# Loading decays whole, queries and keys in two pieces, and four parts of a weight check slice by slice

## The chip, the cores and the metric

One core of a Trainium2 chip runs the whole program. The metric is device time in microseconds for one execution. Lower is better.

## The reference

An attention layer with a complex decay feeds a two-layer network. For each batch, head and time step a state of 48 by 48 is turned and shrunk by the decay, the outer product of key and value is added, and the query reads it:

```python
mag = np.sqrt(a_re * a_re + a_im * a_im)
scale = np.minimum(mag, 0.999) / (mag + 1e-06)
a_re_n, a_im_n = (a_re * scale, a_im * scale)
for t in range(S):                       # S = 768, B = 4, H = 8, D = 48
    new_re = ar * S_re - ai * S_im       # ar, ai: a_re_n, a_im_n at t
    new_im = ar * S_im + ai * S_re
    S_re, S_im = (new_re + kv, new_im)   # kv: outer product of k and v at t
    y[:, :, t] = np.einsum('bhd,bhde->bhe', q[:, :, t], S_re)
h = x @ w_in                             # x: y as 3072 tokens by 384; w_in: 384 x 2048
out = np.maximum(0.01 * h, h) @ w_out    # w_out: 2048 x 384
```

## The kernel before, in words

The recurrence is cut into 12 sub-chunks (`SUBS`) of 128 time steps for two of the four batches. For sub-chunk n the kernel does this:

- `fetch_a(n)` loads the decays (768 KB, two planes: real and imaginary), `fetch_qk(n)` loads the queries and keys (768 KB, two planes), `fetch_v(n)` the values (832 KB). All loads are issued by SP, in one queue.
- `prep(n)` turns decays into running products on ScalarE and VectorE. Its first step is a square of the decays on ScalarE (line 719). Later VectorE multiplies queries and keys by the products into the tile `qkt` (lines 842 and 906).
- `relay_of(n, 0)` and `relay_of(n, 1)` move the queries and then the keys from `qkt` to `t96`, each with five DMAs from SBUF to SBUF, issued by SP (the key relay only after the last step of `prep(n)`).
- `attend(n)` works on TensorE: the scores (many small matmuls, 96 rows by 32 columns of weights), a mask on VectorE, then the product with the values, and the update of the state.

The two-layer network (`forward`) runs between these on TensorE, in groups of 256 tokens: `first` (18 matmuls into `ph`), leaky relu and split on ScalarE and VectorE (`hide`, `halve`), `second` (matmuls into `po`). Its weights come in 64-bit words, and `convert` splits them in the first 90 us.

A last job is `check_weights(i)`: it loads all weights once more, in 11 parts of three slices (part 10 has two), each slice 128 x 384 words of 8 bytes, that is 384 KB, and ScalarE squares them and sums exponentials. The result decides at the end whether a general version has to run. The parts use the two buffers of the tag "a", which the decays used. Part 0 needs `prep(10)` done, part 1 needs `prep(11)`, and part i needs part i - 2 (line 615); so in time the order of loads is 0, 2, 4, 6 and then 1, 8, 3, 10, 5, 7, 9.

The order of instructions on each engine is not written by hand. `drive` simulates the tasks with the cost functions (`dma_cost`, `act_cost` and so on) and picks, for each lane, the task that can start first, by rank. `Lane` then ties each instruction to the one before it on its engine. For a load cut in pieces the kernel replaces the log entries of the pieces by one entry of the whole load (`spq.log[-2:] = [...]`).

`in_turn` (line 579) adds a true wait: the load waits on SP until the load before it in the list `loaded` has landed. `pieces` (line 585) cuts a load into its two planes and puts both in turn; for n < 1 it loads in one piece with no wait. `fetch_a(n)` calls it with n - 1, so that the decays of sub-chunks 0 and 1 come whole and those from 2 on in two; `fetch_qk` cuts from sub-chunk 1 on. Each part of the check is one load of 1152 KB, in turn. While SP waits, everything behind in its queue waits too.

Of the kernel before, what the change touches and what calls it, by code (L numbers as in the profile page):

```python
# [21 lines left out]
P = 128  # L22
# [117 lines left out]
def in_sbuf(x):  # L140
    return x.space == bass.MemoryType.SB
# [42 lines left out]
def dma_cost(name, kw, aps):  # L184
    if name == "memset":
        return 0.3, 0.4
    out = kw["out"]
    if in_sbuf(kw["in_"]) and in_sbuf(out):
        return 0.78, 2.75
    each = out.nbytes() / 400e3  # L190
    return max(each, 0.6), each + 2.4
# [270 lines left out]
def body(ctx, tc, keep, a_in, qk_in, v_in, w_in, out):  # L462
# [26 lines left out]
    spq, plq = Lane(tc, nc.sync, dma_cost), Lane(tc, nc.gpsimd, dma_cost)  # L489
# [15 lines left out]
        out=perm[:, 0].rearrange("p (x r j) -> p x r j", x=NB, r=R),  # L505
        in_=perm[:, 0].rearrange("p (x r j) -> p x r j", x=NB, r=R),
# [3 lines left out]
        out=perm[:, 1].rearrange("p (r j x) -> p r j x", r=R, j=JB),  # L510
        in_=perm[:, 1].rearrange("p (r j x) -> p r j x", r=R, j=JB),
# [28 lines left out]
    a_off = [0]  # L540
# [35 lines left out]

    loaded = []

    def in_turn(x):
        if loaded:  # L580
            landed = mybir.DependencyInfo(mybir.DependencyClass.Sync, mybir.DependencyReason.DATA)
            tc.add_manual_dep(x.ins, loaded[-1], landed, reason="load")
        loaded.append(x.ins.name)

    def pieces(out, in_, n):
        if n < 1:
            spq.dma_start(out=out, in_=in_)
            return
        for l in range(2):
            in_turn(spq.dma_start(out=out[:, l], in_=in_[:, l]))  # L590
        spq.log[-2:] = [dma_cost("dma_start", dict(out=out, in_=in_), [])]

    def fetch_a(n):
        yield "S", *([prepared[n - 2], moved_k[n - 2]] if n > 1 else freed(A) if n else []), *([loading[n - 1]] if n else [])
        N = TI * len(SUBS[n][1]) * C
        loading[n].set(0.0)
        raw_a[n] = a = a_0 if n == 0 else pp.tile([P, 3, N], F32, tag="a", name=f"a_{n}", bufs=2)
        pieces(a[:, 1:3], a_in[a_off[n] : a_off[n + 1]].rearrange("(p l x) -> p l x", p=P, l=2), n - 1)

    def fetch_qk(n):  # L600
        yield "S", *([prepared[n - 1], moved_k[n - 1]] if n else [])
        N = TI * len(SUBS[n][1]) * C
        raw_qk[n] = qk = pp.tile([P, 2, N], F32, tag="qk", name=f"qk_{n}")
        pieces(qk, qk_in[a_off[n] : a_off[n + 1]].rearrange("(p l x) -> p l x", p=P, l=2), n)

    def fetch_v(n):
        yield "S", *(attends_of(n - 1) if n else freed(V))
# [6 lines left out]
    def check_weights(i):  # L614
        yield "S", checked[i - 2] if i > 1 else prepared[nsub - 2 + i]
        s0 = i * WCK
        ns = min(WCK, NWC - s0)
        st = pp.tile([P, WCK, DM], I64, tag="a", name=f"wck_{s0}", bufs=2)
        in_turn(spq.dma_start(out=st[:, :ns], in_=w_in[s0 : s0 + ns].rearrange("s p x -> p s x")))
        words = st.rearrange("p s x -> p (s x)").bitcast(F32).rearrange("p (x two) -> p x two", two=2)  # L620
        lo, hi = words[:, : ns * DM, 0], words[:, : ns * DM, 1]
        yield "A"
        act.activation(lo, hi, AF.Square)
        yield "A"
        act.activation(hi, lo, AF.Exp, scale=-65536.0, accum_out=wacc[:, 1, i : i + 1])
        yield "A"
        act.activation(lo, lo, AF.Exp, scale=40.0, bias=big, accum_out=wacc[:, 0, i : i + 1])

    def freed(*places):
        return [x for x, r in zip(converted, ROUND) if r in places]  # L630
# [723 lines left out]
    for n in range(nsub):  # L1354
        fetched_a[n] = task(fetch_a(n), UNIT[0] + 5.5 * UNIT[1] if n == 1 else R_RELAY + 0.5)
        fetched_qk[n] = task(fetch_qk(n), R_HID if n else UNIT[0] + 2.5 * UNIT[1])
        prepared[n] = task(prep(n), *due(n))
        if n == 0:
            for i in range(NU):
                converted.append(task(convert(i), UNIT[0] + i * UNIT[1]))  # L1360
        fetched_v[n] = task(fetch_v(n), R_RELAY - 1 if n else UNIT[0] + 9.5 * UNIT[1])
        moved_q[n] = task(relay_of(n, 0), R_RELAY)
        moved_k[n] = task(relay_of(n, 1), R_RELAY)
        attended[n] = task(attend(n), R_ATT)
    forwarding = task(forward(), R_FF)
    for i in range(-(-NWC // WCK)):
        checked[i] = task(check_weights(i), R_WCK)
# [87 lines left out]
```

## Time and profile before

| | |
|---|---|
| median of 3 runs | 602.8 us (602.29 to 603.14) |
| the profiled execution | 602.46 us |
| its span in the trace | 600.8 us |
| busy: TensorE (PE), VectorE (DVE), ScalarE (ACT) | 92%, 86%, 66% of the span |
| instruction queue q8 over the span | 61 packets, 1.00 MB |

The span is the time from the first to the last instruction in the trace, so some 1.7 us of the execution lie around it. PE is TensorE's matmuls and PEld its weight loads. SP is the engine that issues nearly all DMAs. "hardware_dynamic" is the queue of data moves that engines issue, and "instruction" those that bring instructions to the engines. "idle ... <-X" says what ended a wait of an engine, and "issue" is time in which it waited for nothing that the profile shows. A releaser can be misattributed when an engine waits for several things.

### The profile page before, as it was taken

Reading aid. Unit: us, or ns where it says so; the run is one execution under the profiler, and the core shown is the slowest. Engines: PE = TensorE matmul, PEld = TensorE weight load, DVE = VectorE, ACT = ScalarE, POOL = GpSimd, SP = SyncE. Lnnn points to the kernel's source line nnn. Section 1 sums busy time; section 2 is a strip of 40 time slices with the busy share of each in tenths; the row PEclk is TensorE's granted clock in tenths of the full one; section 3 lists DMA queues with packets and bytes.
Section 4 is the critical chain, followed back from the end, with each engine's and each line's share of the span. In section 5 each row is a group of like instructions: output and inputs, shape, how many; then the busy total and the mean of one; then the engine's idle time right before and its main releaser. Section 6 shows DMA issues by size and latency. Waiting matters only on the chain.

```text
span 600.8 us, 17929 instructions
## 1 busy us (share of the span) xinstructions
PE 553.6 (92%) x7667; PEld 525.7 (88%) x7667; DVE 514.8 (86%) x880; ACT 399.3 (66%) x882; POOL 5.0 (1%) x23
## 2 busy tenths in 40 slices
PE   3761798999999999999999999999999998999994
PEld 2420488999999999999999999999999998999994
DVE  5999989999889999999999989999999987965232
ACT  7987487495485784582684864764754854687973
POOL 2000000000000000000000000000000000000000
PEclk9995899999999999999999999999999998999998
DMA  8952535325343245223434353153135245446740
GB/s 349 407 190 82 159 96 145 111 70 148 82 137 86 77 138 134 86 80 87 123 89 118 103 132 108 60 132 107 59 80 153 81 123 195 176 138 208 238 159 29
DMA packets 31428, 79.21 MB, mean 132 GB/s; under 512 B 3568, under 2 KB 9712, under 8 KB 31344
## 3 DMA queue, kind: packets, MB, share of 16 engines
q1 hardware_dynamic: 31200, 77.89, 42.7%
q8 instruction: 61, 1.00, 0.7%
q14 instruction: 23, 0.19, 0.1%
q10 hardware_dynamic: 144, 0.13, 0.1%
HBM read 54.26 MB, written 4.72 MB: 98 GB/s over the span
## 4 chain that ended last, share of the span: by engine, by line
PE 83%; DVE 5%; issue 1%; ACT 1%; ACTq 0%; DVEq 0%
PE po L125 33%; PE ph L125 33%; PE att L125 17%; DVE qkt L125 2%; DVE a L125 1%; DVE u L125 1%; DVE stage_st L125 0%; ACT wck L125 0%; DVE stage_hid L125 0%; DVE qk L125 0%; DVE stage_stg L125 0%; DVE scr L125 0%; DVE hid L125 0%; DVE tg L125 0%; ACT ot L125 0%
## 5 line engine op out<-in xcount | busy, mean ns | idle before, releaser
L125 PE MATMUL po<-hid,wout_hi 128*128 128x256 f32 x1152 | 217.4, 281 | 1.8 <-ACT hid L125 1.4
L125 PE MATMUL ph<-x,win_hi 128*128 128x256 f32 x1152 | 217.2, 280 | 0.0
L125 PEld LDWEIGHTS po<-hid,wout_hi 128*128 128x128 f32 x1152 | 182.1, 189 | 6.1 <-issue 3.3
L125 PEld LDWEIGHTS ph<-x,win_hi 128*128 128x128 f32 x1152 | 182.1, 188 | 1.3 <-ACT hid L125 0.4
L125 PE MATMUL ph<-x,win_lo 128*128 128x256 f32 x576 | 142.1, 278 | 0.0
L125 PE MATMUL po<-hid,wout_lo 128*128 128x256 f32 x576 | 139.0, 279 | 0.0
L125 PEld LDWEIGHTS po<-hid,wout_lo 128*128 128x128 f32 x576 | 109.0, 189 | 0.2
L125 PEld LDWEIGHTS ph<-x,win_lo 128*128 128x128 f32 x576 | 108.6, 189 | 0.3
L125 ACT ACTIVATE tg<-ph 128x512 f32<-128x512 f32 x96 | 57.2, 596 | 66.6 <-PE ph L125 64.1
L125 DVE TENSOR_TENSOR tg<-ph,tg 128x512 f32<-128x512 f32 x81 | 55.7, 688 | 30.5 <-ACT tg L125 30.1
L125 DVE TENSOR_TENSOR hid<-tg,hid 128x512 fp32r<-128x512 f32 x81 | 55.6, 687 | 16.5 <-ACT hid L125 16.4
L125 ACT CAST hid<-tg 128x512 fp32r<-128x512 f32 x81 | 49.7, 615 | 25.6 <-DVE tg L125 25.6
L125 DVE TENSOR_TENSOR u<-a 128x384 f32<-128x384 f32 x84 | 46.6, 555 | 1.8 <-ACT a L125 0.4
L125 DVE TENSOR_TENSOR qkt<-qk,a 128x768 f32<-128x768 f32 x48 | 44.5, 953 | 0.1
L125 ACT ACTIVATE rst<-rst,t 96x48 f32<-96x48 f32 x160 | 37.6, 322 | 4.8 <-DVE rst L125 4.8
L125 PE MATMUL att<-t 96*32 96x128 f32 (+3 forms) x1536 | 34.8, 250 | 2.5 <-issue 2.1
L125 PEld LDWEIGHTS att<-t 96*32 96x32 f32 x1536 | 32.4, 144 | 2.6 <-DMA t<-qkt 1.0
L125 PE MATMUL att<-asb,v 128*32 128x128 f32 x592 | 34.2, 285 | 0.0
L125 PE MATMUL att<-t,rst 96*32 96x128 f32 x640 | 33.3, 272 | 0.0
L125 ACT ACTIVATE sq<-a 128x1536 f32<-128x1536 f32 x12 | 17.9, 1489 | 22.6 <-DMA a<-in_a_dram 22.6
L125 ACT ACTIVATE wck<-wck 128x1152 f32<-128x1152 f32 (+1 forms) x22 | 27.0, 1229 | 8.4 <-DMA wck<-in_w_dram 8.3
L125 DVE TENSOR_TENSOR a<-u 128x192 f32<-128x192 f32 x84 | 29.9, 356 | 1.8
(167 smaller groups left out, 797.1 us busy)
## 6 DMA issues: line engine op xcount, KB each, us to landing
t<-qkt SPq DMA_DIRECT2D x48, 290.2 KB, 4.2
wck<-in_w_dram SPq DMA_DIRECT2D x10, 1152.0 KB, 5.6
v<-in_v_dram SPq DMA_DIRECT2D x12, 832.0 KB, 4.5
qk<-in_qk_dram SPq DMA_DIRECT2D x22, 384.0 KB, 3.1
a<-in_a_dram SPq DMA_DIRECT2D x20, 384.0 KB, 3.5
out_dram<-ot SPq DMA_DIRECT2D x11, 384.0 KB, 2.7
t<-qkt SPq DMA_DIRECT2D x24, 129.0 KB, 4.1
stage_st<-in_w_dram SPq DMA_DIRECT2D x3, 768.0 KB, 6.5
```

Of the source, the lines that this page charges most:

```text
L125: x = getattr(self.engine, name)(*args, **kw)
```

## The change

The decays of every sub-chunk are loaded whole, with no wait, and noted in `loaded`. The queries and keys stay in two pieces from sub-chunk 1 on; each waits until the load noted last has landed, and is then noted itself. Of the check, parts 0 to 3 are loaded in single slices, each of which waits until the load two places before it in `loaded` has landed, so that two are in flight. Parts 4 to 10 are loaded whole with no wait but that for their buffer.

```diff
-    def in_turn(x):
-        if loaded:
+    def behind(x, k):
+        if len(loaded) >= k:
             landed = mybir.DependencyInfo(mybir.DependencyClass.Sync, mybir.DependencyReason.DATA)
-            tc.add_manual_dep(x.ins, loaded[-1], landed, reason="load")
+            tc.add_manual_dep(x.ins, loaded[-k], landed, reason="load")
         loaded.append(x.ins.name)
-
-    def pieces(out, in_, n):
-        if n < 1:
-            spq.dma_start(out=out, in_=in_)
-            return
-        for l in range(2):
-            in_turn(spq.dma_start(out=out[:, l], in_=in_[:, l]))
-        spq.log[-2:] = [dma_cost("dma_start", dict(out=out, in_=in_), [])]
 
     def fetch_a(n):
...
-        pieces(a[:, 1:3], a_in[a_off[n] : a_off[n + 1]].rearrange("(p l x) -> p l x", p=P, l=2), n - 1)
+        x = spq.dma_start(
+            out=a[:, 1:3], in_=a_in[a_off[n] : a_off[n + 1]].rearrange("(p l x) -> p l x", p=P, l=2)
+        )
+        loaded.append(x.ins.name)
 
     def fetch_qk(n):
...
-        pieces(qk, qk_in[a_off[n] : a_off[n + 1]].rearrange("(p l x) -> p l x", p=P, l=2), n)
+        src = qk_in[a_off[n] : a_off[n + 1]].rearrange("(p l x) -> p l x", p=P, l=2)
+        if n:
+            for l in range(2):
+                behind(spq.dma_start(out=qk[:, l], in_=src[:, l]), 1)
+            spq.log[-2:] = [dma_cost("dma_start", dict(out=qk, in_=src), [])]
+        else:
+            spq.dma_start(out=qk, in_=src)
...
-        in_turn(spq.dma_start(out=st[:, :ns], in_=w_in[s0 : s0 + ns].rearrange("s p x -> p s x")))
+        src = w_in[s0 : s0 + ns].rearrange("s p x -> p s x")
+        if i < 4:
+            for x in range(ns):
+                behind(spq.dma_start(out=st[:, x], in_=src[:, x]), 2)
+            spq.log[-ns:] = [dma_cost("dma_start", dict(out=st[:, :ns], in_=src), [])]
+        else:
+            spq.dma_start(out=st[:, :ns], in_=src)
```

## Rows read from the trace of the kernel before

**Rows 1.** Page, part 1: busy time, share of the span and instructions of each engine.

```profile
PE 553.6 (92%) x7667; PEld 525.7 (88%) x7667; DVE 514.8 (86%) x880; ACT 399.3 (66%) x882; POOL 5.0 (1%) x23
```

**Rows 2.** All waits of TensorE from 100 to 590 us: total, times, longest.

```profile
PE att L125 <- issue: 2.3, 2, 2.1
```

**Rows 3.** The chain that ended last, near 499 us: start, length, what.

```profile
499.13 2.16 issue
...
501.51 2.86 PE po L125 x12
```

**Rows 4.** The same chain, 36 matmuls of the network in a steady stretch.

```profile
479.39 4.08 PE ph L125 x36
```

**Rows 5.** Stretches: PE, PEld, DVE, ACT, POOL busy; granted clock; DMA share; GB/s.

```profile
501.20:504.40 3.20, 3.11 (x15) 2.96 (x15) 2.72 (x6) 2.95 (x5) 0.00 (x0) 0.50 0.45 136
...
95.10:96.70 1.60, 0.24 (x3) 0.03 (x1) 1.53 (x3) 1.60 (x8) 0.00 (x0) 1.00 0.01 5
96.80:100.00 3.20, 2.83 (x22) 2.63 (x23) 3.08 (x5) 1.58 (x4) 0.00 (x0) 1.00 0.73 165
```

**Rows 6.** DMA queues, 481.5 to 498.8 us, the only queue: packets, MB, share.

```profile
q1 hardware_dynamic: 1439, 2.73, 54.3%
```

**Rows 7.** DMA queues from 498.8 to 499.9 us, the instruction queue.

```profile
q8 instruction: 1, 0.02, 5.4%
```

**Rows 8.** SP's timeline: start and length of issues, tile, source, count.

```profile
423.94 0.33 SPq L125 DMA_DIRECT2D v<-in_v_dram  x1
...
453.72 3.76 SPq L125 DMA_DIRECT2D a<-in_a_dram  x2
...
493.99 0.58 SPq L125 DMA_DIRECT2D wck<-in_w_dram  x1
...
506.34 0.38 SPq L125 DMA_DIRECT2D wck<-in_w_dram  x1
...
539.17 4.00 SPq L125 DMA_DIRECT2D t<-qkt  x5
543.28 17.05 SPq L125 DMA_DIRECT2D wck<-in_w_dram  x4
```

**Rows 9.** DMA queues from 427.9 to 429 us (none before, from 423.9), the instruction queue.

```profile
q8 instruction: 1, 0.02, 5.2%
```

**Rows 10.** DMA queues from 456.6 to 457.7 us (none before, from 453.7), the instruction queue.

```profile
q8 instruction: 1, 0.02, 5.5%
```

**Rows 11.** Page, part 6: DMA issues, KB each, median us from issue to landing.

```profile
v<-in_v_dram SPq DMA_DIRECT2D x12, 832.0 KB, 4.5
qk<-in_qk_dram SPq DMA_DIRECT2D x22, 384.0 KB, 3.1
a<-in_a_dram SPq DMA_DIRECT2D x20, 384.0 KB, 3.5
...
t<-qkt SPq DMA_DIRECT2D x48, 32.2 KB, 2.8
...
wck<-in_w_dram SPq DMA_DIRECT2D x1, 768.0 KB, 4.4
```

**Rows 12.** The chain: the scores of sub-chunk 11.

```profile
546.10 2.74 PE att L125 x93
```

**Rows 13.** Timelines of ScalarE and VectorE from 504 to 515.3 us, three instructions.

```profile
504.03 0.18 ACT L125 ACTIVATION_READ_ACCUMULATOR wck<-wck,low 128x1 f32 x1
512.13 1.27 ACT L125 ACTIVATE wck<-wck 128x1152 f32<-128x1152 f32 x1 [0.60 <-DMA wck<-in_w_dram]
515.29 0.69 DVE L125 TENSOR_TENSOR tg<-ph,tg 128x512 f32<-128x512 f32 x1 [0.84 <-ACT tg L125]
```

**Rows 14.** Waits of ScalarE over the span: total, times, longest.

```profile
ACT sq L125 <- DMA a<-in_a_dram: 22.6, 9, 4.4
```

**Rows 15.** The chain: the scores of sub-chunk 9.

```profile
456.24 3.00 PE att L125 x91
```

**Rows 16.** The chain: 36 matmuls of the network in another stretch.

```profile
301.68 4.24 PE po L125 x36
```

## The prediction before the run

> **What bounds the kernel now.** I read the busy shares first: TensorE works for 92% of the span, more than any other engine [rows 1]. Then its waits from 100 to 590 us, where the change does nearly all its work: there is hardly one but a single stop of 2.1 us that no semaphore ends [rows 2]. So in this stretch a load that lands sooner is worth nothing by itself, and the only things to win are that stop and what hangs on it. The chain puts it at 499.13, inside the scores of sub-chunk 10: 2.16 us of "issue", and behind it 12 matmuls that take 2.86 us [rows 3], where the usual pace is 4.08/36 = 0.113 us each, so 1.36 us [rows 4]. The table by stretches says why those are slow: the granted clock is 0.50 (1.2 of 2.4 GHz) from 501.2 to 504.4, just after the stop [rows 5].
>
> **What the stop is.** TensorE waits for no engine, so I looked at what feeds it. The instruction queue (q8) moves nothing from 481.5 to 498.8, while the data queue is 54.3% busy [rows 6], and its next packet comes in the 1.1 us after that [rows 7]. Check part 0, 1152 KB, had been issued at 493.99 [rows 8]. So TensorE's next instructions moved 4.9 us after that issue, when the part had drained, and TensorE went on at 499.13 + 2.16 = 501.29, some 2.4 us after the block began to move. I read this as a block of instructions queued behind a load on a DMA engine. The same lag shows elsewhere: behind the 832 KB of v issued at 423.94 the block moves at 427.9, 4.0 us later [rows 8, 9]; behind a 384 KB half of the decays issued at 453.72 at 456.6, 2.9 us later [rows 8, 10].
>
> **Part by part.** (The planner's cost of each load is the same before and after, since the log entries are replaced by that of the whole load; so the order on each engine should stay.)
>
> *1. Check part 0 in slices.* Two slices of 384 KB go out at 493.99 and some 0.4 us later, the third when the first has landed, 3.1 to 3.5 us after its issue [rows 11], near 497.3. Behind the waiting third slice SP holds the queries and keys of sub-chunk 11, which waited for the whole part before; that stands within a few tenths. In front of the block lie then 768 KB instead of 1152. No row shows the wait for 768 KB; it lies between 2.9 (384 KB) and 4.0 (832 KB), and since v's landing takes 4.5 and that of the one 768 KB load of the check 4.4 [rows 11] I take 3.8. The block moves at 497.8, TensorE goes on 2.4 later at 500.2: the stop shrinks from 2.16 to 1.1, saved 1.1 us. Ends: 2.0 saved if only the first slice is in front (496.9), 1.3 lost if the block waits for the third slice too (497.3 + 2.9 = 500.2, against 498.9).
>
> *2. The clock behind it.* The 12 matmuls lose 2.86 - 1.36 = 1.5 us [rows 3, 4]. Would a stop of 1.1 us still lower the clock? From 95.1 to 96.7 TensorE was busy 0.24 of 1.6 us and the clock stayed at 1.00 after it [rows 5]. So I take all of it: 1.5 us. Other end: nothing.
>
> *3. How much of 1 + 2 = 2.6 us survives.* TensorE then runs 2.6 us ahead of the other engines. Next in line are the scores of sub-chunk 11 at 546.10 [rows 12]; they need the key relay, whose five moves go out from 539.17 for 4.00 us [rows 8], the last at about 542.6, landing 2.6 to 2.8 later [rows 11], at 545.3: slack 0.8. The relay comes at the end of VectorE's chain, which waits at 515.29 for ScalarE, and ScalarE at 512.13 for check part 2 [rows 13]. Part 2 was issued whole at 506.34 [rows 8]. Now its first slice goes when part 0's last step on ScalarE has freed the buffer, at 504.3 [rows 13]; the second still waits for the second half of the queries and keys, till 506.4; the third goes when the first has landed, 3.1 to 3.5 later, at 507.6, and lands at 511.0, against 512.1. That is 1.1 us sooner, and I add 0.4 for waits that shrink on the way to 539. So the relay gains 1.5, and the scores may start up to 1.5 + 0.8 = 2.3 us sooner: 2.3 of the 2.6 is left.
>
> *4. The decays in one piece.* Ten times a second issue goes and SP no longer sits between the halves, so the decays land 4.4 instead of about 7 us after the issue and the queries follow sooner. What this removes is ScalarE's wait for them, 22.6 us in nine waits [rows 14]; I cost it at nothing, since TensorE shows no wait there [rows 2] and other work of TensorE covers it. But 768 KB instead of 384 now lie before a block of instructions. Where it bites: at 453.72 the block came 2.9 us after the first half and the scores took 3.00 us [rows 10, 15] instead of 2.74 [rows 12], so it was already 0.26 late. With 3.8 it is 0.9 later. This cost is 0 to 0.9 us; most of it would come back out of the stop at 499, whose end is set by a load and not by TensorE. I take 0.2. At the other loads of decays the scores do not stretch, and a block that sat behind the second half (issued 3.4 us later) comes sooner.
>
> *5. The later check parts.* Parts 1 and 3 come as slices after 543.28; parts 4 to 10 go as soon as their buffer is free. ScalarE's order holds the buffer, so there are two in flight at most; TensorE has no wait there [rows 2]: nothing, but see the second rival. Eight more issues on SP of about 0.4 us [rows 8] stand in its idle time. The close behind TensorE's last matmul is unchanged.
>
> **Sum.** 2.3 - 0.2 = 2.1 us off. The profiled execution took 602.46 us (span 600.8 and 1.66 around it), 0.34 below the median of 602.80; so 600.36 for such an execution, 600.7 as a median.
>
> **Rivals.**
> *The block slips in between the slices.* Row: the block did come only when the whole of part 0 had drained [rows 6, 7], but it was one load of 24 rows of 3072 bytes per DMA engine. If each load is an entity, it would now wait for 8 rows: moves at 496.9, TensorE goes on at 499.3, the stop is 0.2 us; 2.0 + 1.5 = 3.5 saved on TensorE, 2.3 to 3.5 behind the relay, say 2.9 and 599.9. The Trainium skill, "DMA: Bandwidth & Descriptors", section "Queues, rings and completion order", says that a DMA engine takes its queues in turn and drains one packet, typically 9 to 17 and at most 64 descriptors, before it goes on to the next. By that rule this rival is right if a slice is a packet; the trace agrees only if all of part 0 was one.
>
> *Part 8 at once, on the other side.* Place: the scores of sub-chunk 11, which eat a block in 2.74 us. Before, part 8 waited for part 1 to land, and the block behind part 1 was in time. Now part 8 (1152 KB) goes 3.7 us after part 1's first slice. If TensorE's request comes after that, the block waits another 4.9 us and moves 8.6 us after the first slice, against some 4 now. The scores start 2 to 2.8 us after that slice (before: 546.10 - 543.28 = 2.8) and run dry at the earliest 2.74 us later [rows 12], so TensorE stands from 5 to 7 until 8.6 + 2.4 = 11: 4 to 6 us, I take 4, and 1.5 for the clock. 602.8 - 2.1 + 5.5 = 606.2. It decides whether the request comes within 3.7 us of the first slice; the request seems to come with the scores' start, so there is a margin of 0.9 us or more, against it.
>
> *Nothing gained.* The stop stays long enough to pull down the clock (third slice in front), or the wait at 457 grows and costs the clock there: 602.8.
>
> *Another pace.* With the clock at 1.00 throughout, 36 matmuls take 4.08 in some stretches and 4.24 in others [rows 4, 16], and I see no cause. Since 471 all run at 4.08. If the 80 us from 510 on flipped, 80 x 0.16/4.08 = 3.1 us would be lost: 602.8 - 2.1 + 3.1 = 603.8. Flips elsewhere can go either way by 1 or 2 us.
>
> **How the numbers follow.** What can be told from no change is 0.2%, 1.2 us. Forecast 0.46, slip between slices 0.20, nothing gained 0.17, part 8 at once 0.07, pace lost 0.10. Faster by over 0.2%: the first two, 0.66. Within: 0.20, the third and some of the last. Slower: 0.14. The range runs from the slip case with all its 3.5 us and a lucky flip of 1 us, 598.3, to near the lost pace, 603.5.
>
> **What would show it.** Right: the stop near 499 shorter than 1.3 us and no stretch at 0.50 after it; the block of instructions moving before 498; scores of sub-chunk 9 near 3.5 to 3.9 us; those of sub-chunk 11 starting about 2 us sooner, perhaps after a short wait for the relay. Wrong: a stop of 2 us or more at 499, at 457 or at 546, or 36 matmuls at 4.24 after 510. ScalarE's waits for the decays should fall from 22.6 to under 10 us without effect on the time.

## The result and the profile after

The change made the kernel slower: 607.29 us as a median of 11 runs (604.18 to 610.92) against 603.23 for the kernel before beside it (602.29 to 605.90), a ratio of 1.0064 with a 95% interval of 1.0039 to 1.0089. That is 3.9 us, three times what can be told from no change; 600.7 had been forecast, and 603.5 was the upper end of the range. The profiled execution is the longest of the 11: 610.92 us with a span of 609.2, 8.4 us above the span before. So its rows show each loss, but some are larger than in a usual run.

TensorE's waits from 100 to 590 us, which answer to [rows 2]:

```profile
PE po L125 <- ACT hid L125: 3.3, 1, 3.3
PE att L125 <- issue: 1.5, 3, 0.8
PE ph L125 <- ACT x L125: 0.7, 1, 0.7
PE ph L125 <- DVE tg L125: 0.5, 1, 0.5
```

The stop of 2.1 us near 499 is gone, and waits for other engines, which were absent, sum to 4.5 us. The table by stretches (columns as in [rows 5]) places the cost behind the longest:

```profile
499.00:504.40 5.40, 5.40 (x75) 5.27 (x78) 4.49 (x10) 1.56 (x2) 0.00 (x0) 1.00 0.37 99
507.00:519.70 12.70, 10.20 (x89) 9.96 (x84) 7.80 (x21) 7.23 (x17) 0.00 (x0) 0.99 0.62 192
519.70:526.50 6.80, 6.00 (x28) 6.00 (x29) 6.80 (x8) 3.34 (x9) 0.00 (x0) 0.51 0.51 176
```

Behind 499 the granted clock now stays at 1.00, where it had been 0.50 [rows 5]. But from 519.7 to 526.5 it is at 0.51 (1.2 GHz), behind a stretch in which TensorE stood for 2.5 of 12.7 us. Here 6.00 us of busy time are about twice what the same work would take at 2.4 GHz, so I estimate 3.0 us lost.

The chain that ended last says where the wait comes from (start, length, what):

```profile
493.77 5.35 DMA wck<-in_w_dram
...
499.14 3.56 DMA wck<-in_w_dram
...
507.31 3.84 DMA wck<-in_w_dram
...
511.18 3.87 DMA wck<-in_w_dram
...
519.94 0.52 ACT hid L125
520.46 0.04 issue
520.50 4.21 PE po L125 x18
```

Each of parts 0 and 2 of the check is two landings one behind the other: the third slice goes out only at 499.14 and 511.18, when the first has landed. The key relay, at the end of VectorE's chain, goes out at 542.51, against 539.17 before [rows 8]. ScalarE works in order, so while it waits for a part it does nothing for TensorE. Its timeline:

```profile
502.81 2.79 ACT L125 ACTIVATE wck<-wck 128x1152 f32<-128x1152 f32 x2 [5.18 <-DMA wck<-in_w_dram]
515.15 2.56 ACT L125 ACTIVATE wck<-wck 128x1152 f32<-128x1152 f32 x2 [4.68 <-DMA wck<-in_w_dram]
```

Before, part 2 was squared from 512.13 after 0.60 us [rows 13], and part 0 came 2.8 us sooner, by the same view of the kernel before:

```profile
500.04 2.58 ACT L125 ACTIVATE wck<-wck 128x1152 f32<-128x1152 f32 x2 [2.25 <-DMA wck<-in_w_dram]
```

A second loss stands where the prediction had put nothing, at the very end. The last piece of the chain is the compare that writes `bad`, and behind it every engine jumps over the general version. The last row of the chain, before:

```profile
597.64 0.15 DVE bad L125
```

and in the changed kernel:

```profile
603.49 0.15 DVE bad L125
```

The DMA queues (packets, MB, share) from that row's end to the end of the span, before:

```profile
q14 instruction: 3, 0.02, 3.1%
```

and in the changed kernel:

```profile
q14 instruction: 4, 0.03, 1.8%
```

The span ends 600.8 - 597.79 = 3.0 us after the compare before, and 609.2 - 603.64 = 5.6 us now: 2.5 us more, with a fourth packet on the second instruction queue, q14. One of the four comes in the last 3.2 us, when the other three are through (the queues from 606 to 609.2):

```profile
q14 instruction: 1, 0.01, 1.0%
```

So the 8.4 us of the two profiles are: 3.7 gained behind 499 (stop and clock, [rows 3, 4]), 4.5 lost in waits, 3.0 in the clock, 2.5 at the close, and 2.1 left over. At least part of that is pace: 18 matmuls take 2.12 us on the changed chain at 534, 0.118 us each, against 0.113 in [rows 4].

```profile
533.98 2.12 PE po L125 x18
```

A third, smaller loss is the stop of 0.8 us inside the scores of sub-chunk 9 at 457.74, behind the decays that now come whole. It is among the "issue" waits above, and so in the 2.1 left over.

### The profile page after: what moved, and what is told of

Read it like the earlier page. It is cut to its first block, busy times and chain, and to the rows that moved or that the text cites. A ratio compares the mean times of both kernels' runs of the same rounds, so it can differ in the third digit from the quotient of the medians.

```text
span 609.2 us, 17911 instructions
## 1 busy us (share of the span) xinstructions
PE 556.0 (91%) x7667; PEld 528.4 (87%) x7667; DVE 514.1 (84%) x880; ACT 400.1 (66%) x882; POOL 5.0 (1%) x23
## 4 chain that ended last, share of the span: by engine, by line
PE 71%; DMA 6%; DVE 6%; ACT 5%; issue 1%; SPq 1%; ACTq 0%; DVEq 0%
PE ph L125 28%; PE po L125 28%; PE att L125 15%; DMA wck<-in_w_dram 5%; ACT wck L125 3%; DVE qkt L125 2%; SPq L125 1%; DMA t<-qkt 1%; DVE a L125 1%; DVE hid L125 1%; DVE tg L125 1%; ACT a L125 0%; ACT tg L125 0%; DVE qk L125 0%; ACT hid L125 0%
## 5 line engine op out<-in xcount | busy, mean ns | idle before, releaser
L125 PE MATMUL att<-t 96*32 96x128 f32 (+3 forms) x1536 | 36.3, 257 | 2.5 <-DMA t<-qkt 1.7
L125 PEld LDWEIGHTS att<-t 96*32 96x32 f32 x1536 | 33.9, 145 | 4.7 <-DMA t<-qkt 2.2
L125 ACT CAST hid<-ph 128x512 fp32r<-128x512 f32 x30 | 17.5, 587 | 15.4 <-PE ph L125 10.3
```

The costliest lines, as they stand in the source:

```text
L125: x = getattr(self.engine, name)(*args, **kw)
```

## The experiments

My theory on seeing this was that the wait between the slices is the whole loss. The rivals: the whole decays; slices as such; the later parts with no wait. All runs were timed against the kernel before on the same chip.

### One half of the change at a time

The fetches as changed, the check as before:

```diff
-        if i < 4:
-            for x in range(ns):
-                behind(spq.dma_start(out=st[:, x], in_=src[:, x]), 2)
...
+        behind(spq.dma_start(out=st[:, :ns], in_=src), 1)
```

> Decays, queries and keys are loaded as in the changed kernel; every part of the check is whole and in turn, as before. Theory (the wait between slices): the loss sits in the check, so this stands within 0.3% of before, 602 to 605 us, with the stop of about 2 us near 499 and the clock at 0.50 behind it still there, and ScalarE's wait for part 2 about 0.6 us. Rival (the whole decays, or what they do to the queries behind them): 606 to 608 us, like the changed kernel, with TensorE waiting for ScalarE near 520.

Measured: 605.84 us, ratio 1.0050 (1.0031 to 1.0070). My theory had 602 to 605, so it fell: most of the loss came without a single slice. The rival's 606 to 608 was missed by little, but TensorE does not wait for ScalarE near 520, so its mechanism was not there either. The stop near 499 with the low clock behind it is there as before. What is new in its profile: a longer stop behind the whole decays and the long close (604.6 - 599.46 = 5.1 us). The chain at 457:

```profile
454.44 2.74 PE att L125 x88
457.18 1.44 issue
458.62 0.32 PE att L125 x3
458.95 1.77 PE ph L125 x9
```

The 9 matmuls behind the stop take 1.77 us, and 1.24 in the run with two pieces below: the clock fell here as well. The DMA queues from 452 to 456.2 us, where this is the only one that moves anything, and those from 456.2 to 457 tell why TensorE stands:

```profile
q1 hardware_dynamic: 308, 0.96, 70.5%
```

```profile
q8 instruction: 1, 0.02, 7.5%
```

The decays were issued at 451.95 and the block of instructions moved only after 456.2, more than 4.2 us later, when they had drained.

The check as changed, the fetches as before:

```diff
-        in_turn(spq.dma_start(out=st[:, :ns], in_=w_in[s0 : s0 + ns].rearrange("s p x -> p s x")))
+        if i < 4:
+            for x in range(ns):
+                behind(spq.dma_start(out=st[:, x], in_=src[:, x]), 2)
...
+        else:
+            spq.dma_start(out=st[:, :ns], in_=src)
```

> Decays, queries and keys are loaded as before, in two pieces in turn; the check is as in the changed kernel. Theory (the wait between slices): nearly the whole loss is here, 605.5 to 608 us; part 0 lands about 9 us after its first slice was issued instead of 6, ScalarE waits 4 to 5 us each for parts 0, 2 and 1, and TensorE waits 2 us or more for ScalarE near 520, with the clock at 0.50 behind that. Rival (the whole decays): 602 to 604 us.

Measured: 603.73 us, 1.0023 (1.0005 to 1.0041): slower, but by 1.4 us and not by the whole loss. That is the rival's range, not my 605.5 to 608. The late parts are there (ScalarE waits 3.5 and 4.6 us for parts 0 and 2), the stop at 499 is down to 0.9, and TensorE waits for ScalarE, 0.8 us near 517 and 1.3 us near 554, without a fall of the clock:

```profile
PE ph L125 <- ACT x L125: 1.3, 1, 1.3
PE att L125 <- issue: 0.9, 1, 0.9
PE po L125 <- ACT hid L125: 0.8, 1, 0.8
```

The close is 600.4 - 597.44 = 3.0 us. The two halves together, 3.0 + 1.4 = 4.4 us by their ratios, make up the 3.9 of the whole within the intervals.

### Slices without a wait, and no slices

Slices with no wait:

```diff
-                behind(spq.dma_start(out=st[:, x], in_=src[:, x]), 2)
+                loaded.append(spq.dma_start(out=st[:, x], in_=src[:, x]).ins.name)
```

> The changed kernel, but the slices of parts 0 to 3 are issued one behind the other with no wait for a landing. Theory (the wait between slices): parts 0 and 2 land 6 to 6.5 us after the first issue, ScalarE's waits for them fall to about 2.5 and 1 us, TensorE's wait for ScalarE near 520 and the low clock behind it go, and the time is 600 to 604 us; the stop near 499 comes back in part, 0.5 to 2.2 us, since 1152 KB stand before the block of instructions again. Rival (slices as such, by their number or size): 606 to 608 us, the waits stay. Rival (parts 4 to 10 with no wait): the wait near 520 goes, but 2 us or more are lost behind 550.

Every part whole and at once:

```diff
-        if i < 4:
...
+        loaded.append(spq.dma_start(out=st[:, :ns], in_=src).ins.name)
```

> The changed kernel, but every part of the check is one load with no wait but that for its buffer. Theory (the wait between slices): as with slices that do not wait, 600 to 604 us, no wait of TensorE for ScalarE near 520. It goes one step further than the run with slices that do not wait: if that one is slow and this one fast, it is the slices as such; if both are fast, it is the wait; if both are slow, it is either the whole decays or parts 4 to 10 at once, which the first two runs tell apart.

Measured: 606.57 us, 1.0062 (1.0042 to 1.0083), and 607.38 us, 1.0095 (1.0068 to 1.0122). Both missed my 600 to 604. TensorE's wait for ScalarE near 520 did go in both, as the theory said (the first has one of 1.1 near 557); but in the first the stop at 499 was 0.9 and a stop of 1.0 stood at 459, and in the second they were 2.1 and 1.1, with a third of 1.3 at 550. Both closes are long, 5.0 and 5.4 us. By now all four kernels with whole decays had the long close with four packets on q14, and the two without had the short one.

### The close

First guess: with fewer instructions on SP, its code behind the jump lies across two blocks. Code that is never entered can move that place:

```diff
         nc.vector.memset(S2, 0.0)
+        pad = ga.tile([P, 1], F32, tag="pad", name="pad")
+        for _ in range(11):
+            nc.sync.dma_start(out=pad, in_=nat[0, 0:P, 0:1])
```

> The changed kernel with eleven small DMAs on SP added in front of the general version's loop, which no run enters: nothing that is executed changes, only where SP's code behind the jump over the general version lies. In the first four runs the kernels with whole decays took 5.1 to 5.6 us from the end of the last piece of the chain (the compare that writes bad) to the end of the span, with a fourth packet of the second instruction queue (q14) late in it; before and the run with only the check changed took 3.0, with three. New theory (the close): with whole decays SP has some ten instructions less, its code behind the jump lies across two blocks, and one more block is fetched at the very end. Then this close falls to about 3.0 us with three packets, and the time to 604.5 to 605.5 us, 2.0 to 2.5 below the changed kernel. Rival (the close follows from something executed, or from ScalarE's code): the close stays above 5 us and the time at 606.5 to 608.

The counterpart on ScalarE:

```diff
...
+        for _ in range(9):
+            nc.scalar.copy(pad, pad)
```

> The counterpart: the changed kernel with nine copies on ScalarE added in the general version, which no run enters, so that ScalarE's code is as long as before and SP's stays as it was. If it is SP's code that makes the close long, the close stays above 5 us with four packets of q14 and the time at 606.5 to 608; if it is ScalarE's, the close is 3.0 us here and the time 604.5 to 605.5.

Measured: 607.07 us, 1.0051 (1.0024 to 1.0079), close 606.3 - 600.77 = 5.5 us; and 607.54 us, 1.0063 (1.0040 to 1.0086), close 5.8. Both have four packets, and the first missed my 604.5 to 605.5. So the place behind the jump, on either engine, is not it. What these two share with the changed kernel is what SP runs through before the jump. Where the close is short, one more packet of q14 had come earlier; the queues from 560 to 590 us of the kernel before hold it, and those of the changed kernel from 560 to 600 hold none:

```profile
q14 instruction: 1, 0.01, 0.1%
```

Second guess, then: SP asks for its next block when it reaches a certain place in its code. With some ten executed instructions less, it gets there only at the end. Two kernels give SP instructions back, in different places. The decays as two pieces with no wait between them:

```diff
...
+            for l in range(2):
+                x = spq.dma_start(out=a[:, 1 + l], in_=src[:, l])
```

> The changed kernel, but the decays of sub-chunks 2 to 11 go out as two pieces, one right behind the other with no wait: the same 768 KB lie in the queue, and SP runs through as many instructions as in the kernel before (nine more than the changed kernel). In the runs so far the fourth late packet of q14 came exactly where SP has nine or more executed instructions less than before, whatever lies behind the jump, and in the others a packet came at 557 to 575 us instead. New theory (SP reaches the instruction at which its next block is asked for only at the very end): the close falls to 3.0 to 3.5 us, three packets of q14 at the end and one near 575, and the time is 604.5 to 605.8 us, about 2.2 below the changed kernel. Rival (the close hangs on the whole decays or on what they do to other engines): close above 5 us, 606.5 to 608. On the stop near 457: if it is the bytes in front of the block of instructions that count, it is 0.8 to 1.6 us as with the whole decays; if a block can slip in between two loads, it is 0.3 or less, and the time 1 us lower still.

And parts 4 to 10 in slices, the decays whole as in the change:

```diff
         else:
-            spq.dma_start(out=st[:, :ns], in_=src)
+            for x in range(ns):
+                spq.dma_start(out=st[:, x], in_=src[:, x])
...
```

> The changed kernel, but parts 4 to 10 of the check go out in slices too, with no wait: the same loads at the same time, and SP runs through thirteen instructions more. Theory (SP's place in its code): the close is 3.0 to 3.5 us, with three packets of q14 at the end, and the time 604.5 to 605.8 us. Rival (the whole decays make the close long): above 5 us, 606.5 to 608.

Measured: 603.18 us, 1.0025 (1.0005 to 1.0044), close 600.4 - 597.43 = 3.0; and 604.20 us, 1.0041 (1.0017 to 1.0065), close 601.3 - 598.40 = 2.9. Both times lie a little below the 604.5 to 605.8 I had given. Both have three packets behind the compare, and the early one, too, at 574.6 and 571.8. The packets behind the compare in the first:

```profile
q14 instruction: 3, 0.02, 3.0%
```

All 14 profiles of this case fall in line: the close is 5.0 to 5.8 us with four packets in the six kernels with the changed kernel's SP work or less, and 2.9 to 3.0 with three in the eight others. The time came down by 0.39% and 0.23% of the ratio, 2.4 and 1.4 us, each known to about 2, and in the first run the stop at 457 went as well; the close is shorter by 2.0 to 2.9. These two runs show that the number of instructions SP runs through before the jump switches the close. That it does so by the place at which SP asks for its next block is the guess that fits, and is not shown: which of the packets is SP's, the trace does not say.

The first of the two also bears on the other question put to it. From 450 us on its chain has no stop in the scores of sub-chunk 9:

```profile
454.27 1.06 PE ph L125 x9
455.33 2.95 PE att L125 x92
458.28 1.24 PE ph L125 x9
```

The same 768 KB lay in the queue, issued from 452.80, as two loads. The block moved from 454.4 on, 1.6 to 1.8 us after the first piece's issue, and before all had drained: from 452.8 to 454.4 only 0.25 MB of data had moved,

```profile
q1 hardware_dynamic: 189, 0.25, 72.8%
```

and the block came in the 0.2 us behind:

```profile
q8 instruction: 1, 0.02, 31.3%
```

In the seven profiles with whole decays and TensorE's code where it was, the stop was 0.8 to 1.7 us; here it is 0.2. Its lag is that behind a half that went out alone (1.6 to 2.9 us, in three profiles with the decays as before). So in this run the block did not wait for all the bytes in the queue. The Trainium skill, "DMA: Bandwidth & Descriptors", section "Queues, rings and completion order", says that a DMA engine takes its queues in turn, a packet at a time. This profile agrees if a whole load counts as one packet and each piece as a packet of its own; it is one profile, and the slices of part 0 do not bear it out as plainly (see the part on the prediction). When TensorE asks for a block, no trace records.

### The stop at 499 without the check

The kernel before, with TensorE's code moved: the 16 matmuls of the mask are done three times over at the start, with the same result.

```diff
+        n = len(pe.log)
+        for _ in range(3):
...
+        del pe.log[n + 16 :]
```

> The kernel before, with the 16 matmuls that make the mask done three times over at the start, where TensorE waits for the first weights anyway: the borders of TensorE's blocks of instructions lie 128 instructions earlier in the work, all else is as it was. Theory (the stop at 499 is a block of instructions that has to wait for part 0 because its request comes after that load's issue): the request for this block now comes some microseconds ahead of part 0, the stop of 2.16 us and the 0.50 clock behind it go, TensorE is 3 to 4 us ahead at 507, and the time is 598.5 to 601.5 us, unless another block now meets a load. Rival (TensorE cannot keep such a lead, since ScalarE and VectorE are late next): 601.5 to 603 us, with new waits of TensorE for them by 525.

Measured: 601.95 us, 0.9973 (0.9952 to 0.9995): faster than both kernels, the only one of this study that is. It lies in the rival's 601.5 to 603, not in my 598.5 to 601.5: of the 3.7 us of stop and low clock some 1.6 are kept (0.3 to 2.9 by the interval). The stop is gone, and TensorE's "issue" waits fall from 2.3 to 0.6 us:

```profile
PE att L125 <- issue: 0.6, 2, 0.3
PE ph L125 <- ACT x L125: 0.3, 1, 0.3
```

So the stop comes where a border of TensorE's code meets a load, and the load's size alone does not make it: here part 0 was whole.

### Which parts of the check eat the gain

Part 0 alone in slices, all else as before:

```diff
-        in_turn(spq.dma_start(out=st[:, :ns], in_=w_in[s0 : s0 + ns].rearrange("s p x -> p s x")))
+        if not i:
+            for x in range(ns):
+                behind(spq.dma_start(out=st[:, x], in_=src[:, x]), 2)
...
+        else:
+            behind(spq.dma_start(out=st[:, :ns], in_=src), 1)
```

> The kernel before, with part 0 of the check alone in three slices, two in flight; parts 1 to 10 whole and in turn, decays, queries and keys as before. With all of the check as in the changed kernel TensorE was 3.8 us ahead at 505 and lost it all by 568. Theory (late parts 1 to 3 eat it): part 0's slices take the stop away, parts 2, 1 and 3 land as before, and a third or more of the 3.8 us is kept: 600 to 602 us. Rival (part 0 itself is late, and what ScalarE waits for it is what eats the gain): 602.5 to 604.5 us, as with all four parts in slices.

Measured: 603.49 us, 0.9996 (0.9972 to 1.0019). That is the rival's range, not my 600 to 602: no gain that can be told, no loss either. In its profile a stop of 1.1 us is left near 499 and one of 1.2 stands behind 540, so it did not take the stop away whole and doesn't separate the theories well.

The other test adds the shift of TensorE's code to the changed kernel with the short close (parts 4 to 10 in slices). The edit is that of both runs above.

> The run with parts 4 to 10 in slices, and the 16 matmuls of the mask done three times over at the start, as in the run that shifted the blocks of TensorE. Theory (what the change costs is where borders of code fall: the close, and a block of instructions behind the whole decays near 457): the stop near 457 goes too, and the time is 602 to 604.5 us, within 0.2% of before. Rival (the whole decays or the slices cost time by themselves): 605 us or more, with waits of TensorE for other engines.

Measured: 605.98 us, 1.0074 (1.0050 to 1.0098): the rival's number. Here nothing is left of either stop or of the long close (2.9 us), and the kernel is still slower. Its waits, and the stretch behind 520:

```profile
PE po L125 <- ACT hid L125: 2.2, 1, 2.2
...
PE att L125 <- issue: 0.3, 1, 0.3
```

```profile
517.00:520.00 3.00, 0.78 (x7) 0.58 (x7) 2.31 (x3) 3.00 (x9) 0.00 (x0) 1.00 0.02 7
520.00:527.00 7.00, 7.00 (x47) 7.00 (x48) 7.00 (x10) 3.44 (x7) 0.00 (x0) 0.76 0.64 225
```

TensorE does 0.78 us of work from 517 to 520, ScalarE being busy all the time, and the clock falls to 0.50 behind that (0.76 on average over the second stretch). To tell slices from decays, the same kernel with parts 0 to 3 whole again and the decays as two pieces:

```diff
         if i < 4:
-            for x in range(ns):
-                behind(spq.dma_start(out=st[:, x], in_=src[:, x]), 2)
+            behind(spq.dma_start(out=st[:, :ns], in_=src), 1)
```

> The run with TensorE's blocks shifted and parts 4 to 10 in slices, but with parts 0 to 3 whole again, each waiting for the load before it as in the kernel before, and with the decays as two pieces back to back (so that SP's number of instructions keeps the close short). In that run the stops at 457 and 499 were gone, TensorE was 3 us ahead at 505 and then lost it all near 520 in waits for ScalarE (3.7 us, two waits) and a clock at 0.50 behind them. Theory (the slices of parts 0 and 2 land late and hold ScalarE): here TensorE's waits for ScalarE are 1.7 us or less, as where the kernel before was shifted, no stretch at 0.50 follows near 520, and the time is 600 to 603 us. Rival (the whole decays, or a TensorE that runs ahead by 3 us whatever the slices): waits of 3 us or more and 605 us or more.

Measured: 602.84 us, 0.9997 (0.9973 to 1.0020), inside the theory's 600 to 603. The same two stretches:

```profile
517.00:520.00 3.00, 3.00 (x29) 3.00 (x28) 3.00 (x4) 0.95 (x2) 0.00 (x0) 1.00 0.69 224
520.00:527.00 7.00, 7.00 (x62) 6.83 (x61) 6.04 (x8) 5.53 (x9) 0.00 (x0) 1.00 0.51 161
```

TensorE is busy throughout and ScalarE only for 0.95 us of the first stretch: it got its parts of the check 1.3 and 2.4 us sooner and was done with them. ScalarE's first step of parts 0 and 2, with the slices:

```profile
501.99 2.62 ACT L125 ACTIVATE wck<-wck 128x1152 f32<-128x1152 f32 x2 [3.39 <-DMA wck<-in_w_dram]
514.60 2.48 ACT L125 ACTIVATE wck<-wck 128x1152 f32<-128x1152 f32 x2 [5.21 <-DMA wck<-in_w_dram]
```

and with whole parts:

```profile
500.68 2.60 ACT L125 ACTIVATE wck<-wck 128x1152 f32<-128x1152 f32 x2 [1.78 <-DMA wck<-in_w_dram]
512.17 2.49 ACT L125 ACTIVATE wck<-wck 128x1152 f32<-128x1152 f32 x2 [3.28 <-DMA wck<-in_w_dram]
```

So the slices of parts 0 to 3 cost time by themselves once TensorE runs ahead. How much of that is the landing that the third slice waits for is not shown: without that wait part 0 still came 6.7 us after its first slice's issue, against 5.8 to 6.1 when whole. Parts 4 to 10 with no wait are in this run as well, so they cost nothing that can be told. The decays' form changed in this run too; with the stop at 457 gone from both, they have no known way to cost the difference, but that was not run apart.

## Why the prediction was wrong

The sign was wrong, and three steps failed. Against the forecast, items 1 to 3 weigh most: 2.3 us gained was forecast, and the run with the check alone lost 1.4, a swing of 3.7. The close comes next with 2.2, then the decays with 0.6.

**The close.** "The close behind TensorE's last matmul is unchanged" (item 5): it is 2.0 to 2.9 us longer. The fewer instructions of SP were counted as time on SP, never as a place in its code. Nothing in the rows before pointed at it but the packet of q14 near 575, which I had not read.

**Items 1 and 3, the third slice.** The sum had it issued "when the first has landed, 3.1 to 3.5 us after its issue, near 497.3", from the landing time of a lone 384 KB load [rows 11]. By its own figures the third slice would then land at 500.4 to 500.8, later than the 500.04 at which part 0 was squared before; yet item 3 kept ScalarE's end of part 0 at 504.3. With two slices in flight, and the key relay's moves just in front, the first took 5.35 us in the profiled run (3.4 to 4.3 in the seven other profiles in which the third slice waits), and the third went out at 499.14. Part 0 was squared at 502.81 instead of 500.04. That is 9.0 us after the first issue; the seven others have 6.8 to 7.6, and whole parts 5.8 to 6.1. The queries and keys of sub-chunk 11, which I had "within a few tenths", went out at 502.72, behind that slice. For part 2 I had a landing at 511.0; ScalarE got it at 515.15. So the key relay, forecast 1.5 us sooner, went out 3.3 us later, and TensorE waited for ScalarE, in the kernels with parts 0 to 3 in slices 0.9 to 3.3 us at the longest. Behind the three longest of these waits (3.3, 2.2 and 2.1 us) the clock fell.

**Item 4, the whole decays.** The mechanism was right and the size was off: I took 0.2 us of a range of 0 to 0.9, and the stop was 0.8 to 1.7 us in seven profiles. In two of them the clock fell behind it, which I had put under "nothing gained". That it "would come back out of the stop at 499" was wrong in the profile of the changed kernel, which has no such stop to come out of.

What held: the stop at 499 is a block of instructions that waits behind part 0, and slices shorten it. In the profile of the changed kernel the rival had it right, not the forecast: the block slipped in between the slices. In the first 1.4 us after the first slice's issue, 493.77 to 495.2, when 0.22 MB had moved, the instruction queue's packet is there already:

```profile
q1 hardware_dynamic: 184, 0.22, 65.3%
q8 instruction: 1, 0.02, 10.6%
```

But that was this one profile. Seven others have part 0 in the same slices and TensorE's code where it was. In them the block moved 3.7 to 4.5 us after the first slice's issue, close to the 3.8 that item 1 took, and the stop was 0.5 to 1.7 us, against 1.1 forecast. The queues of the run with the check alone, from 492.37 to 496.1 (nothing else moved) and from 496.1 to 496.3:

```profile
q1 hardware_dynamic: 446, 0.95, 76.9%
```

```profile
q8 instruction: 1, 0.02, 29.1%
```

So the size of item 1 was right in these seven. Its reason, the bytes in front, is not shown: in the run with no wait all three slices were issued before the block moved, and it came after 3.7 us there, too, not after the 4.9 of the whole part. Why it came sooner still in the profile of the changed kernel stays open. The gain of 1.5 us at the clock (item 2) is not bound to the stop's length alone: in the run with every part at once the stop is 2.1 us, as before, and the granted clock behind it stays at 1.00 (columns as in [rows 5]):

```profile
499.90:502.10 2.20, 0.07 (x2) 0.00 (x0) 1.24 (x3) 1.29 (x2) 0.00 (x0) 1.00 0.18 42
502.10:505.50 3.40, 3.40 (x30) 3.31 (x30) 3.02 (x7) 2.72 (x4) 0.00 (x0) 1.00 0.50 139
```

ScalarE's waits for the decays fell from 22.6 to 8.3 us and bought nothing, as said. Part 8 at once did no harm in the changed kernel: TensorE has no stop near 546 there. The other pace came in the profiled run, for some 2 us at most; what sets it is still open. What 3.9 us are made of, by the runs: about 2.2 of close, about 0.8 from the decays (3.0 of the run with the fetches alone less 2.2), and about 1.4 from the check, within intervals of about 1 us each. They sum to 4.4.

## What to carry to other kernels

A load cut in pieces can let instructions through sooner, and the pieces need no wait for that: behind two loads of the decays back to back a block came after less than 1.8 us, against 3.8 to 4.7 behind the whole load; behind part 0 in slices it mostly came after 3.7 to 4.5, against 4.9 to 5.0. The slices cost in turn: with a wait for a landing between them the whole part came 0.7 to 1.8 us later in seven profiles and 3.0 in an eighth, and the engine that works in order behind it pays. And before a DMA or a wait is added or taken away, look at when each engine's instruction blocks come, to the very last one: a change of some ten instructions moved the end of this kernel by over 2 us.

## What was not expected of the hardware

- The end of the span hangs on how many instructions SP has run through: 2.9 to 3.0 us or 5.0 to 5.8 us behind the same compare.
- A block of instructions waited more than 4.2 us behind one load of 768 KB and less than 1.8 us behind the first of two loads of 384 KB with the second right behind it. Behind the first of two slices of part 0 in flight, 384 KB each, the range over eight profiles was 1.3 to 4.5 us.
- The clock fell to 0.50 for 6.8 us behind a wait of 3.3 us, and stayed at 1.00 behind one of 1.3. But it fell behind a stop of 1.4 us in the run with the fetches alone, and stayed at 1.00 behind one of 2.1 in the run with every part at once.
- One kernel scatters by about 1% from run to run: the changed one from 604.18 to 610.92, and the kernel before, 602.29 to 605.90 beside it, from 598.89 to 606.65 in 35 runs on another chip.
